# Attention, gated MLP and routed experts on one core: SyncE's transfers written into the hand-laid order, and the second pass's partial sums kept in DRAM until the third

## The chip, the cores and the metric

The kernel runs on one core of one Trainium2 chip. The metric is the device time of one execution in microseconds (us); three executions of the kernel before gave 585.97, 586.28 and 587.97 us, median 586.28.

## What is computed

Three layers follow one another on 1536 tokens (2 sequences of 768) of 512 features. The reference, cut to what matters:

```python
scores = scale * q @ k.T - slope[h] * dist            # 8 heads of 64
keep   = (pos_k < n_global) | (0 <= pos_q - pos_k < n_local)   # 8 global keys, 96 local ones
x   = softmax(where(keep, scores, -1e9)) @ v          # attention
h   = x @ w_in                                        # 512 -> 2048
x2  = (h * tanh(softplus(h))) @ w_out                 # 2048 -> 512
e   = argmax(x2 @ w_gate)                             # one of 8 experts per token
out = gate * relu(x2 @ w1[e]) @ w2[e]                 # 512 -> 1024 -> 512
```

## The kernel before, in words

**Attention.** Tokens are taken in 12 tiles of 128 (t). A step s is half a tile's heads (s = 2t or 2t+1). `a_S` makes the scores of four heads on PE (tile `sp`), `a_max` adds bias and takes the row maximum on DVE (M), `a_exp` takes the exponential on ACT (E), `a_T` transposes on PE (T, tile `pt`), `a_Tev` copies the transposes out of PSUM on ACT (C, tile `PT`), `a_V` multiplies by the values on PE (V, tile `av`). Then `a_n` scales by the row sums on DVE (N), `a_X` transposes the tile (X, tile `xp`), and `a_xh` and `a_xl` split it into a high and a low part in the rounded 32-bit type (h on ACT, l on DVE). Two tiles make a block b of 256 tokens.

**MLP.** Each product is three matmuls (high·high, high·low, low·high). The 2048 inner features are taken in 8 pairs of 128, j, and in three passes, `PASSES = [(0, 1), (2, 3), (4, 5, 6, 7)]`. A unit (pass, block, j) is a first matmul group `L1_mms` (tile `hp`, 24 matmuls), eleven small steps of `mish` (m, alternating ACT and DVE), and a second matmul group `L2_mms` (tile `acc`, 12 matmuls) that runs two units behind the first. The weights come as 64-bit floats and are converted in 32 chunks: `load_raw` (a transfer of 512 KB into tile `wst`), then `conv_raw` in parts c (three integer operations on DVE, tile `cv`), d (a cast on ACT) and e (a subtraction on DVE).

**Partial sums.** At the end of the first pass's units for a block, `acc_evac` (through `evac0`, line 506) copies the two accumulators out on ACT and SyncE writes them to DRAM (`xps`). In the second pass `part_load` (line 500) has read them back, DVE adds them to the accumulators in PSUM (line 529), and SyncE writes the sums (line 530). In the third pass they are read again and DVE adds them once more (line 522); the result goes to the router and to the expert layer.

**What sets the order.** A string of tokens, `ORDER`, lays attention, the first ten units' L1 (L), their mish steps, the first eight units' L2 (G) and 14 of the 32 conversions by hand. Inside this "loop" PE, ACT, DVE and POOL issue exactly as the tokens stand (`manual_schedule`). SyncE (SP) is not in that list: its transfers are placed by the compiler's scheduler, some called out of tokens (`scores`, `v_end`, `half1`). The buffers bound it: six staging buffers `stp` shared by query tiles and raw weights, two `vv` for the values. Each transfer on SP also waits for the eighth one before it to have landed, as eight semaphores are used in turn. After the loop the units run from a Python loop, and the scheduler orders all engines. `prefill` writes 24 pieces of zero rows into the experts' table `xg` in units 14 to 21.

The lines of that loop which the change touches:

```python
if p > 0 and j == PASSES[p][0]:
    part_load(b)
...
if u <= NU and jl == PASSES[pl][-1]:
    acc_evac(u - 2)
if 14 <= u < 22:
    for _ in range(CAPMAX // 112):
        next(zero_rows, None)
```

Of the kernel before, what the change touches and what calls it, by code (L numbers as in the profile page):

```python
# [22 lines left out]
TPB = S // 128  # L23
# [20 lines left out]
def moe_kernel(ctx, tc, q, k, v, n_global, n_local, w_in, w_out, w_gate, w1, w2, out, dbg=None):  # L44
# [12 lines left out]
    xps = dr.tile([NT, DM], F32, name="xps")  # L57
# [171 lines left out]
    def load_qk(t, n=2):  # L229
        b, i = divmod(t, TPB)  # L230
        c0 = NG + (i // 2) * KB + (i % 2) * 128
        w = n * 128
        nc.sync.dma_start(kT[:, :, c0:c0 + w], k_t[:, :, t * 128:t * 128 + w])
        qr = stp.tile([128, 4, w], F32, tag="st", name="qr")
        nc.sync.dma_start(qr, q_t[:, :, t * 128:t * 128 + w])
        for j in range(n):
            qkt[t + j] = qr[:, :, j * 128:(j + 1) * 128]

    def load_v(t):
        b, i = divmod(t, TPB)  # L240
        s0 = i * 128
        vv = at.tile([128, 2, DM], F32, tag="vv", name="vv")

        def ld(r0, n, col, tok):
            nc.sync.dma_start(vv[r0:r0 + n, col], v[b * S + tok:b * S + tok + n, :])

        if i == 0:
            ld(0, 128, 1, 0)
            nc.gpsimd.memset(vv[0:KR, 0], 0.0)
            ld(0, NG, 0, 0)  # L250
        elif i % 2 == 0:
            ld(0, NL, 0, s0 - NL)
# [141 lines left out]
    def a_xl(t):  # L394
# [8 lines left out]
        if o == 1:  # L403
            for c, xx in enumerate((xh, xl)):
                nc.sync.dma_start(xs[blk, c], xx.rearrange("p k t -> p (k t)").bitcast(F32))
# [89 lines left out]
    def part_load(b):  # L495
        xpl[b] = []
        for o in range(2):
            t = 2 * b + o
            xp = xe.tile([128, DM], F32, tag="xp", name="xpl", bufs=4)
            nc.sync.dma_start(xp, xps[t * 128:(t + 1) * 128, :])  # L500
            xpl[b].append(xp)

    def evac0(b, o):
        t = 2 * b + o
        xp = xe.tile([128, DM], F32, tag="xp", name="xpo", bufs=4)
        nc.scalar.copy(xp, accs[b][o])
        nc.sync.dma_start(xps[t * 128:(t + 1) * 128, :], xp)
        if o == 1:
            del accs[b]

    def acc_evac(u):
        p, b, j = units[u]
        if p == 0:
            evac0(b, 0)
            evac0(b, 1)
            return
        ac = accs.pop(b)
        for o in range(2):
            t = 2 * b + o
            if p == 2:  # L520
                x2 = xe.tile([128, ROW], F32, tag="x2", name="x2")
                nc.vector.tensor_add(x2[:, 0:DM], ac[o], xpl[b][o])
                nc.gpsimd.tensor_copy(x2[:, DM:DM + 1], tokid[:, t:t + 1])
                xes[t] = x2
                if "x2" in dbg:
                    nc.sync.dma_start(dbg["x2"][t * 128:(t + 1) * 128, :], x2[:, 0:DM])
            else:
                xp = xpl[b][o]
                nc.vector.tensor_add(xp, ac[o], xp)
                nc.sync.dma_start(xps[t * 128:(t + 1) * 128, :], xp)  # L530
# [75 lines left out]
    def prefill():  # L606
# [4 lines left out]
        for e in range(NE):  # L611
            for c in range(CAPMAX // 112):
                r0 = e * ERS + c * 112
                tc.keep_in_program_order(nc.sync.dma_start(xg[r0:r0 + 112, :], z))
                yield

    zero_rows = prefill()
# [234 lines left out]
    q0 b0 q1 S0 S1 M0.0 q2 M1.0 M1.1 E0.0 M0.1 S2 M0.2 E1.0 M0.3 M1.2 E0.1 M1.3 b1 E0.2 E0.3 b2 E1.1 T0.0 E1.2 c0  # L852
    T0.1 E1.3 C0.0 T1.0 C0.1 T1.1 q3 V0 M2.0 d0 c1 C1.0 S3 E2.0 C1.1 M3.0 d1 V1 M2.1 E3.0 p2 M2.2 M3.1 E2.1 M2.3
# [510 lines left out]
```

## Time and profile before

| | us |
|---|---|
| median of 3 runs | 586.28 |
| the profiled execution: its time | 586.55 |
| the profiled execution: its span, first to last instruction | 584.8 |
| PE busy | 563.5 (96% of the span) |
| DVE busy | 471.6 (81%) |
| ACT busy | 374.2 (64%) |
| the loop's last G on PE ends, and the units behind it begin | about 138 |
| the third pass ends, about | 362 |

The span and the execution's own time differ by 1.75 us, which lies around the instructions. Matmuls are pipelined, so a PE that counts as busy need not be at its full rate; the time between the starts of two rows tells more. The trace counts each 32-bit matmul of attention as two instructions, so what the order prints as x8 stands as x16 there. A few matmul records are missing, so counts in a row can be a little low.

### The profile page before, as it was taken

How to read it: one execution, taken by the hardware profiler on the slowest of the kernel's cores; microseconds unless marked ns; L12 is line 12 of the kernel's file. 1: busy time of each engine (PE TensorE's matmuls, PEld its weight loads, DVE VectorE, ACT ScalarE, POOL GpSimd, SP SyncE). 2: the span in 40 equal slices, each digit the busy share in tenths (PEclk: the TensorE clock that was granted, in tenths of full speed). 3: DMA queues.
4: the chain of work that ended last, by engine and by line, in shares of the span. 5: the costliest groups of instructions: out<-in, count | busy, mean ns of one | idle time of the engine just before them, and what ended most of it. 6: DMA issues, size and time to landing. Idle time of an engine off the chain costs nothing.

```text
span 584.8 us, 12654 instructions
## 1 busy us (share of the span) xinstructions
PE 563.5 (96%) x4650; PEld 519.9 (89%) x4650; DVE 471.6 (81%) x1141; ACT 374.2 (64%) x878; POOL 84.6 (14%) x156
## 2 busy tenths in 40 slices
PE   6998999999999998999999999899999999999994
PEld 5898899988898987999898898699999999999994
DVE  7899988899999999877776677485966778898942
ACT  6898899786666556554555645376655556776731
POOL 2204010010100100102111110122210302212111
PEclk9899999999999999999999999999999999999997
DMA  8998455556999994412232200838749276577200
GB/s 251 324 324 251 169 166 187 190 169 236 324 345 319 326 252 162 145 36 91 67 116 89 74 20 19 277 133 294 268 148 319 84 272 221 180 287 255 95 19 22
DMA packets 54654, 110.00 MB, mean 188 GB/s; under 512 B 5440, under 2 KB 12608, under 8 KB 54583
## 3 DMA queue, kind: packets, MB, share of 16 engines
q1 hardware_dynamic: 48882, 90.21, 46.7%
q0 software_dynamic: 5696, 18.89, 9.7%
q8 instruction: 38, 0.62, 0.4%
q14 instruction: 34, 0.27, 0.1%
q10 hardware_dynamic: 4, 0.00, 0.0%
HBM read 84.67 MB, written 25.10 MB: 188 GB/s over the span
## 4 chain that ended last, share of the span: by engine, by line
PE 77%; DVE 11%; DMA 4%; issue 3%; ACT 2%; SPq 1%; POOL 1%; DVEq 0%; POOLq 0%; ACTq 0%
PE hp L429 19%; PE acc L448 19%; PE bacc L721 6%; PE bhp L721 6%; PE av L367 3%; PE bacc L722 3%; PE bhp L722 3%; PE sp L301 3%; PE bhp L724 1%; PE bacc L724 1%; PE bacc L726 1%; PE bhp L725 1%; PE bacc L725 1%; PE bhp L726 1%; DMA xg<-x,dsi 1%
## 5 line engine op out<-in xcount | busy, mean ns | idle before, releaser
L448 PE MATMUL acc<-wpair,gh 128*128 128x512 f32 x384 | 120.7, 398 | 4.2 <-ACT gh L485 4.2
L429 PE MATMUL hp<-xh,wpair 128*128 128x256 f32 x768 | 118.4, 285 | 0.0
L429 PEld LDWEIGHTS hp<-xh,wpair 128*128 128x128 f32 x768 | 104.5, 188 | 3.9 <-ACT P L325 0.3
L448 PEld LDWEIGHTS acc<-wpair,gh 128*128 128x128 f32 x384 | 67.8, 188 | 16.9 <-ACT gh L485 5.4
L161 DVE TENSOR_TENSOR bw<-bst,bw 128x512 fp32r<-128x512 f32 x112 | 72.9, 685 | 10.0 <-ACT bw L160 9.5
L160 ACT CAST bw<-bst 128x512 fp32r<-128x512 f32 x112 | 64.3, 619 | 19.3 <-PE bhp L725 9.6
L448 PE MATMUL acc<-wpair,gl 128*128 128x512 f32 x192 | 74.6, 394 | 0.0
L456 ACT ACTIVATE e<-hp 128x512 f32<-128x512 f32 x48 | 28.6, 596 | 54.6 <-PE hp L429 54.6
L429 PE MATMUL hp<-xl,wpair 128*128 128x256 f32 x384 | 62.0, 282 | 0.0
L721 PE MATMUL bhp<-xc,bw 128*128 128x352 f32 (+4 forms) x192 | 59.3, 364 | 0.7 <-DVE t L756 0.6
L721 PE MATMUL bacc<-hc,bw 128*128 128x352 f32 (+4 forms) x192 | 59.2, 364 | 0.0
L429 PEld LDWEIGHTS hp<-xl,wpair 128*128 128x128 f32 x384 | 52.7, 188 | 0.8 <-issue 0.3
L722 PE MATMUL bhp<-xc,bw 128*128 128x176 f32 (+4 forms) x192 | 48.5, 253 | 0.0
L722 PE MATMUL bacc<-hc,bw 128*128 128x176 f32 (+4 forms) x192 | 48.3, 252 | 0.0
L325 ACT ACTIVATE P<-P,mx 128x232 f32<-128x232 f32 (+1 forms) x96 | 44.7, 472 | 3.1 <-DVE mx L314 2.9
L460 ACT ACTIVATE n<-e 128x512 f32<-128x512 f32 x48 | 30.4, 633 | 21.6 <-DVE e L458 19.8
L466 DVE SCALAR_TENSOR_TENSOR n<-n,r 128x512 f32<-128x512 f32 x48 | 32.9, 685 | 13.9 <-ACT r L464 13.3
L448 PEld LDWEIGHTS acc<-wpair,gl 128*128 128x128 f32 x192 | 35.7, 188 | 7.8 <-DVE gl L488 0.4
L488 DVE SCALAR_TENSOR_TENSOR gl<-n,gh 128x512 fp32r<-128x512 f32 x48 | 32.8, 686 | 9.4 <-ACT gh L485 8.6
L721 PEld LDWEIGHTS bhp<-xc,bw 128*128 128x128 f32 x192 | 36.1, 188 | 1.7 <-DVE t L756 0.8
L722 PEld LDWEIGHTS bhp<-xc,bw 128*128 128x128 f32 x192 | 36.7, 191 | 0.0
L722 PEld LDWEIGHTS bacc<-hc,bw 128*128 128x128 f32 x192 | 36.7, 191 | 0.0
(190 smaller groups left out, 1218.4 us busy)
## 6 DMA issues: line engine op xcount, KB each, us to landing
bst<-in_moe_w_dram SPq DMA_DIRECT2D x56, 512.0 KB, 6.4
wst<-in_moe_w_in_dram SPq DMA_DIRECT2D x16, 512.0 KB
wst<-in_moe_w_out_dram SPq DMA_DIRECT2D x16, 512.0 KB, 5.1
xh<-xs POOLq DMA_DIRECT2D x12, 512.0 KB, 5.5
xl<-xs POOLq DMA_DIRECT2D x12, 512.0 KB, 4.8
xpl<-xps SPq DMA_DIRECT2D x24, 256.0 KB, 4.4
xg<-z SPq DMA_DIRECT2D x24, 224.9 KB, 8.3
w0f<-in_moe_w_dram SPq DMA_DIRECT2D x8, 512.0 KB, 8.2
```

Of the source, the lines that this page charges most:

```text
L160: nc.scalar.copy(hi, src)
L161: nc.vector.tensor_sub(lo, src, hi.bitcast(F32))
L301: nc.tensor.matmul(sps[s][j][:, i, 0:w], lhsT=qkt[t][r, 2 * pr + i, :], rhs=kT[r, 2 * pr + i, k0:k0 + w], start=True, stop=True)
L325: nc.scalar.activation(out=Ps[s][:, q_, 0:w], in_=Ps[s][:, q_, 0:w], func=AF.Exp, bias=mxs[s][:, q_:q_ + 1], scale=-1.0, accum_out=rcs[t][ ...
L429: yield lambda f=f, kk=kk, wi=wi, xx=xx, cs=cs: nc.tensor.matmul(hp[:, f, :], lhsT=w[:, wi, kk, cs], rhs=xx[:, kk, :], start=(kk == 0 and ...
L448: yield lambda f=f, o=o, cs=cs, gi=gi, wi=wi, first=first, last=last: nc.tensor.matmul(accs[b][o], lhsT=gi[:, cs], rhs=w[:, wi, f, :], sta ...
L456: nc.scalar.activation(out=e, in_=hp, func=AF.Exp, scale=-1.0)
L460: nc.scalar.activation(out=n, in_=e, func=AF.Square)
L466: nc.vector.scalar_tensor_tensor(out=n, in0=n, scalar=0.25, in1=r, op0=ALU.add, op1=ALU.mult)
L488: nc.vector.scalar_tensor_tensor(out=gl, in0=n, scalar=-(2.0 ** -80), in1=gh.bitcast(F32), op0=ALU.mult, op1=ALU.subtract)
L721: nc.tensor.matmul(o[:, 0:2 * cap], lhsT=wh, rhs=xc, start=first, stop=False)
L722: nc.tensor.matmul(o[:, 0:cap], lhsT=wl, rhs=xh, start=False, stop=last)
```

## The change

SP joins the engines that `ORDER` lays out, and the string is written anew, with new tokens: K and Q (keys and queries of a tile or of two), W (values), w (a raw weight chunk), x (a block's high and low parts to DRAM), y (a partial sum to DRAM), z (a piece of zero rows) and u (clearing a value buffer). The opening's value buffer is cleared by DVE instead of POOL. `zero_tile` is made at token k, and all 24 zero pieces are written inside the loop instead of in units 14 to 21. `xps` has room for two partial sums per token. Both the first and the second pass copy their accumulators out on ACT and write them; nothing is loaded or added in the second pass. In the third pass `part_load` reads two tiles per half block at the third unit of four, `part_sum` adds them at the fourth, and one addition to the accumulator is left, as before.

```diff
-    xps = dr.tile([NT, DM], F32, name="xps")
+    xps = dr.tile([2, NT, DM], F32, name="xps")
...
-    def load_qk(t, n=2):
...
+    def load_k(t):
+        n = 1 if t < 2 else 2
...
+        nc.sync.dma_start(kT[:, :, c0:c0 + n * 128], k_t[:, :, t * 128:(t + n) * 128])
+
+    def load_q(t):
+        n = 1 if t < 2 else 2
+        qr = stp.tile([128, 4, n * 128], F32, tag="st", name="qr")
+        nc.sync.dma_start(qr, q_t[:, :, t * 128:(t + n) * 128])
...
+    def zero_v(t, eng):
+        vvt[t] = at.tile([128, 2, DM], F32, tag="vv", name="vv")
+        eng.memset(vvt[t][0:KR, 0], 0.0)
...
         if i == 0:
+            ld(0, NG, 0, 0)
             ld(0, 128, 1, 0)
-            nc.gpsimd.memset(vv[0:KR, 0], 0.0)
-            ld(0, NG, 0, 0)
...
+            xpl[b].append([xe.tile([128, DM], F32, tag="xp", name="xpl", bufs=4) for _ in range(2)])
+            for p, xp in enumerate(xpl[b][o]):
+                nc.sync.dma_start(xp, xps[p, t * 128:(t + 1) * 128, :])
+
+    def part_sum(b):
+        for x0, x1 in xpl[b]:
+            nc.vector.tensor_add(x0, x0, x1)
...
+    def evac_store(p, b, o):
+        t = 2 * b + o
+        nc.sync.dma_start(xps[p, t * 128:(t + 1) * 128, :], evs.pop((b, o)))
+
     def acc_evac(u):
         p, b, j = units[u]
-        if p == 0:
-            evac0(b, 0)
-            evac0(b, 1)
+        if p < 2:
+            for o in range(2):
+                evac0(b, o)
+                evac_store(p, b, o)
             return
...
-                xp = xpl[b][o]
-                nc.vector.tensor_add(xp, ac[o], xp)
-                nc.sync.dma_start(xps[t * 128:(t + 1) * 128, :], xp)
...
     ORDER = """
-    q0 b0 q1 S0 S1 M0.0 q2 M1.0 M1.1 E0.0 M0.1 S2 M0.2 E1.0 M0.3 M1.2 E0.1 M1.3 b1 E0.2 E0.3 b2 E1.1 T0.0 E1.2 c0
...
+    K0 Q0 Q1 K1 Q2 q1 q0 b0 q2 S0 w0 q3 S1 S2 M0.0 M0.1 W0 E0.0 M1.0 S3 M0.2 E0.1 M1.1 M1.2 K2 E1.0 M0.3 M1.3 E0.2
...
-    with tc.manual_schedule(engines={mybir.EngineType.PE, mybir.EngineType.Activation, mybir.EngineType.DVE, mybir.EngineType.Pool}), tc.tile_pool(name="tmp0", bufs=1, side="right") as tmp0:
+    with tc.manual_schedule(engines={mybir.EngineType.PE, mybir.EngineType.Activation, mybir.EngineType.DVE, mybir.EngineType.Pool, mybir.EngineType.SP}), tc.tile_pool(name="tmp0", bufs=1, side="right") as tmp0:
...
-            if p > 0 and j == PASSES[p][0]:
+            if p == 2 and j == PASSES[p][2]:
                 part_load(b)
+            if p == 2 and j == PASSES[p][3]:
+                part_sum(b)
...
-        if 14 <= u < 22:
-            for _ in range(CAPMAX // 112):
-                next(zero_rows, None)
```

SyncE's first transfers, before the change (kT, qr and vv are keys, queries and values; wst is a raw weight chunk):

```order
L233 DMA kT<-in_k_dram 128x4x128
L235 DMA qr<-in_q_dram 128x4x128
L233 DMA kT<-in_k_dram 128x4x128
L235 DMA qr<-in_q_dram 128x4x128
L245 DMA vv<-in_v_dram 128x512
L185 DMA wst<-in_moe_w_in_dram 128x2x512 x2
L245 DMA vv<-in_v_dram 104x512
L245 DMA vv<-in_v_dram 120x512
L245 DMA vv<-in_v_dram 8x512 x2
L233 DMA kT<-in_k_dram 128x4x256
L235 DMA qr<-in_q_dram 128x4x256
```

And with the change:

```order
L233 DMA kT<-in_k_dram 128x4x128
L238 DMA qr<-in_q_dram 128x4x128 x2
L233 DMA kT<-in_k_dram 128x4x128
L238 DMA qr<-in_q_dram 128x4x256
L185 DMA wst<-in_moe_w_in_dram 128x2x512
L254 DMA vv<-in_v_dram 8x512
L254 DMA vv<-in_v_dram 128x512
L233 DMA kT<-in_k_dram 128x4x256
```

The second query tile is now third, one raw chunk stands ahead of the first values instead of two, the eight global rows of the values come first of the values, and the keys of tiles 2 and 3 follow at once.

PE's first rows of attention before (sp: S, pt: T, av: V):

```order
L301 MATMUL sp<-kT,qr 128x136 x8
L301 MATMUL sp<-kT,qr 128x232 x4
L337 MATMUL pt<-ident,P 72x128 x4
L339 MATMUL pt<-ident,P 128x128 x4
L337 MATMUL pt<-ident,P 72x128 x4
L339 MATMUL pt<-ident,P 128x128 x4
L367 MATMUL av<-vv,PT 64x64 x16
L301 MATMUL sp<-kT,qr 128x232 x4
L367 MATMUL av<-vv,PT 64x64 x16
L301 MATMUL sp<-kT,qr 128x232 x8
```

And with the change:

```order
L308 MATMUL sp<-kT,qr 128x136 x8
L308 MATMUL sp<-kT,qr 128x232 x8
L344 MATMUL pt<-ident,P 72x128 x4
L346 MATMUL pt<-ident,P 128x128 x4
L344 MATMUL pt<-ident,P 72x128 x4
L346 MATMUL pt<-ident,P 128x128 x4
L374 MATMUL av<-vv,PT 64x64 x16
L308 MATMUL sp<-kT,qr 128x232 x4
L344 MATMUL pt<-ident,P 104x128 x4
L346 MATMUL pt<-ident,P 128x128 x4
L374 MATMUL av<-vv,PT 64x64 x16
```

One more group of wide scores stands ahead of the first transposes; behind the first V comes S4 (tile 2), whose keys are the last transfer shown above.

DVE in the second pass before, a piece with one of its six pairs of additions (L529):

```order
L175 SCALAR_TENSOR_TENSOR cv<-wst,cv 128x512
L529 TENSOR_TENSOR xpl<-acc,xpl 128x512
L488 SCALAR_TENSOR_TENSOR gl<-n,gh 128x512
L211 TENSOR_TENSOR wpair_2_2947<-cv,wpair_2_2947 128x512
L529 TENSOR_TENSOR xpl<-acc,xpl 128x512
L466 SCALAR_TENSOR_TENSOR n<-n,r 128x512
```

And ACT in the second pass with the change, where the copies stand between steps of mish:

```order
L470 ACTIVATE r<-n,cqs 128x512
L519 COPY xpo<-acc 128x512
L472 ACTIVATE r<-r 128x512
L493 ACTIVATE gh<-n 128x512
L519 COPY xpo<-acc 128x512
L464 ACTIVATE e<-hp 128x512
```

All twelve of DVE's additions leave the second pass, and ACT copies twelve accumulator halves there.

## Rows read from the trace of the kernel before

**Rows 1.** Busy time by stretch: length, PE, PEld, DVE, ACT, POOL, PEclk, DMA, GB/s.
```profile
15.00:20.00 5.00, 5.00 (x58) 4.23 (x56) 3.37 (x18) 3.28 (x14) 2.04 (x2) 0.66 1.07 369
...
60.00:138.00 78.00, 77.83 (x895) 69.42 (x894) 72.08 (x196) 66.89 (x177) 4.08 (x8) 1.00 0.52 171
138.00:192.00 54.00, 54.00 (x351) 49.31 (x349) 53.88 (x99) 35.93 (x63) 4.34 (x8) 1.00 0.98 329
192.00:226.00 34.00, 31.28 (x195) 27.47 (x194) 33.95 (x62) 19.89 (x33) 3.45 (x6) 1.00 0.91 273
...
240.00:360.00 120.00, 120.00 (x917) 108.12 (x916) 86.51 (x187) 66.62 (x125) 15.77 (x25) 1.00 0.22 71
```

**Rows 2.** PE's timeline, opening: start, us, engine, line, what, [idle before <-releaser].
```profile
6.00 1.20 PE L301 MATMUL sp<-kT,qr 64*128 64x136 f32 x16
...
12.31 0.34 PE L367 MATMUL av<-vv,PT 128*64 128x64 f32 x4 [0.21 <-ACT PT L352]
14.05 1.03 PE L367 MATMUL av<-vv,PT 72*64 72x64 f32 x28 [1.40 <-DMA vv<-in_v_dram]
15.02 1.56 PE L301 MATMUL sp<-kT,qr 64*128 64x232 f32 x8
...
18.41 2.03 PE L301 MATMUL sp<-kT,qr 64*128 64x232 f32 x16
```

**Rows 3.** The chain that ended last, pieces at PE's full rate: start, us, what.
```profile
22.76 2.01 PE av L367 x64
...
30.94 1.77 PE sp L301 x16
...
80.18 0.87 PE pt L339 x8
```

**Rows 4.** ACT's timeline in the opening.
```profile
7.48 0.69 ACT L275 ACTIVATE qr<-qr,qsc 128x128 f32<-128x128 f32 x2 [1.42 <-DMA qr<-in_q_dram]
...
11.22 1.04 ACT L352 COPY PT<-pt 72x512 f32<-72x512 f32 x2
```

**Rows 5.** DVE's timeline in the opening: its wait for the two integers.
```profile
3.83 0.19 DVE L71 CAST int_f<-int_raw 1x4 f32<-1x4 int32 x1 [0.70 <-DMA int_raw<-in_n_global_dram]
```

**Rows 6.** PE's timeline inside the loop.
```profile
46.55 0.64 PE L429 MATMUL hp<-xl,wpair 128*128 128x256 f32 x4
48.85 0.66 PE L339 MATMUL pt<-ident,P 128*128 128x128 f32 x4 [1.65 <-DVE xl L398]
...
64.24 0.65 PE L385 MATMUL xp<-ident,xn 128*128 128x128 f32 x4 [0.17 <-DVE xn L378]
```

**Rows 7.** The timeline of POOL and DVE ahead of that wait.
```profile
44.69 2.22 POOL L270 TENSOR_TENSOR qr<-qr,qsc 128x512 f32<-128x512 f32 x2
...
46.05 1.41 DVE L173 SCALAR_TENSOR_TENSOR cv<-wst,cv 128x512 int32<-128x512 int32 x1
...
47.50 0.69 DVE L175 SCALAR_TENSOR_TENSOR cv<-wst,cv 128x512 int32<-128x512 int32 x1
```

**Rows 8.** The chain that ended last, second pass.
```profile
186.63 2.77 PE acc L448 x12
189.39 2.90 PE hp L429 x24
...
235.49 2.76 PE acc L448 x12
```

**Rows 9.** PE's timeline, the longest wait of the second pass.
```profile
223.94 1.19 PE L448 MATMUL acc<-wpair,gh 128*128 128x512 f32 x4 [2.10 <-ACT gh L485]
```

**Rows 10.** Line 529 alone: count, ns min/median/max, first and last start.
```profile
L529 DVE TENSOR_TENSOR xpl<-acc,xpl x12: 673/678/692, 172.1 to 234.0; 128x512 f32<-128x512 f32 x12
```

**Rows 11.** Groups of instructions: busy us, mean ns of one, idle before.
```profile
L470 DVE TENSOR_TENSOR e<-e,r 128x512 f32<-128x512 f32 x48 | 32.9, 686 | 0.7
...
L506 ACT COPY xpo<-acc 128x512 f32<-128x512 f32 x12 | 6.5, 582 | 0.0
```

**Rows 12.** The page's part 6, transfers: count, KB each, median us to landing.
```profile
xg<-z SPq DMA_DIRECT2D x24, 224.9 KB, 8.3
```

More of the change, by code (lines that the diff above doesn't have):

```diff
@@ L241, in load_v @@
         s0 = i * 128
-        vv = at.tile([128, 2, DM], F32, tag="vv", name="vv")
+        if i:
+            vvt[t] = at.tile([128, 2, DM], F32, tag="vv", name="vv")
+        vv = vvt[t]
         def ld(r0, n, col, tok):
@@ L402, in a_xl, with x_store @@
                                   xx[:, :, cs].bitcast(F32))
-        if o == 1:
-            for c, xx in enumerate((xh, xl)):
-                nc.sync.dma_start(xs[blk, c], xx.rearrange("p k t -> p (k t)").bitcast(F32))
+    def x_store(blk):
+        for c, xx in enumerate(xT[blk]):
+            nc.sync.dma_start(xs[blk, c], xx.rearrange("p k t -> p (k t)").bitcast(F32))
     def x_reload(blk):
@@ L519, in acc_evac @@
             t = 2 * b + o
[L520 to L527, printed above, removed]
-                xp = xpl[b][o]
-                nc.vector.tensor_add(xp, ac[o], xp)
-                nc.sync.dma_start(xps[t * 128:(t + 1) * 128, :], xp)
+            x2 = xe.tile([128, ROW], F32, tag="x2", name="x2")
+            nc.vector.tensor_add(x2[:, 0:DM], ac[o], xpl[b][o][0])
+            nc.gpsimd.tensor_copy(x2[:, DM:DM + 1], tokid[:, t:t + 1])
+            xes[t] = x2
+            if "x2" in dbg:
+                nc.sync.dma_start(dbg["x2"][t * 128:(t + 1) * 128, :], x2[:, 0:DM])
     dsi_ins = [None]
@@ L610, in prefill, with zero_rows @@
         nc.gpsimd.memset(z[:, DM + 1:ROW], 0.0)
[L611 to L617, printed above, removed]
+        zt.append(z)
+    def zero_rows(i):
+        e, c = divmod(i, CAPMAX // 112)
+        r0 = e * ERS + c * 112
+        nc.sync.dma_start(xg[r0:r0 + 112, :], zt[0])
     cnt = const.tile([1, NE], F32, name="cnt")
@@ L934, in moe_kernel, with first_k @@
         l2 = [L2_mms(u) for u in range(LOOPU)]
-        def v_end(s):
-            a_V(s)
-            if s % 2 and s // 2 + 2 < NTILE:
-                load_v(s // 2 + 2)
-        def scores(s):
-            a_S(s)
-            if s % 4 == 3 and 1 < s // 2 // 2 + 2 + 0 < NTILE // 2 and s > 3:
-                load_qk(2 * (s // 4) + 4)
-        def half1(c):
-            next_conv(0)
-            next_raw()
+        def first_k():
+            load_k(0)
+            prep_qk(0)
         def consts(_):
@@ L952, in consts @@
             build_consts(tmp0)
[L954 removed]
+            zero_tile()
+        todo = {
             "b": lambda a: bias(a), "q": lambda s: scale_q(int(s)), "p": lambda t: prep_qk(int(t)),
[L956 removed]
+            "S": lambda s: a_S(int(s)), "V": lambda s: a_V(int(s)), "R": lambda t: a_rec(int(t)),
             "N": lambda t: a_n(int(t)), "X": lambda t: a_X(int(t)), "h": lambda t: a_xh(int(t)),
[L958 to L959 removed]
+            "l": lambda t: a_xl(int(t)), "c": lambda c: next_conv(0), "d": lambda c: next_conv(1),
+            "e": lambda c: next_conv(2), "k": consts,
             "M": lambda s, q_: a_max(int(s), int(q_)), "E": lambda s, q_: a_exp(int(s), int(q_)),
```

102 lines of the change are left out of this document (43 added, 59 removed).

## The prediction

> **What bounds the kernel now.** I read the page's first part, which makes PE the busiest engine, then busy time by stretch, then PE's timeline and the chain of waits where a stretch showed a gap. In most stretches PE has no gap at all: from 138 to 192 and from 240 to 360 it is busy all the time, from 60 to 138 for 77.83 of 78 us [rows 1]. So a change to the order can only win what PE loses, and three places show a loss that this change touches.
>
> The first is the opening. From the first scores at 6.00 to 18.41, 12.41 us, PE does sixteen narrow scores (1.20), sixteen wide ones, sixteen transposes and 64 av instructions [rows 2]. At PE's full rate the wide scores take 1.77, the av 2.01 and the transposes 2 x 0.87 = 1.74 [rows 3], together 6.72 with the narrow ones; so 5.7 are lost. They fall in three parts. Up to 12.31: 6.31 us for 1.20 + 0.885 + 1.74 = 3.8 of work, 2.5 lost, because ACT's scalings of the second query tile begin at 7.48 and its exponentials, which the transposes wait for, last to 11.22 [rows 4]. From 12.31 to 15.02: 2.71 for 1.0 of av, 1.7 lost, mostly to the values' transfer [rows 2]. From 15.02 to 18.41: 3.39 for 0.885 + 1.0, 1.5 lost with no wait; the granted clock is 0.66 there, the mean of a stretch at 2.4 and one at 1.2 GHz [rows 1].
>
> The second is one wait inside the loop: four matmuls at 46.55 take until 48.85, where four of that kind take 2.90 / 6 = 0.48 at full rate [rows 6, 8], so 1.8 are lost. PE waits for DVE's `xl`; ahead of it a conversion step of DVE took 1.41 instead of about 0.69 beside a POOL multiply [rows 7].
>
> The third is the second pass. DVE is busy for 53.88 of 54 and 33.95 of 34 us [rows 1], and PE falls behind it: 2.72 us idle between 192 and 226, the longest wait 2.10 [rows 1, 9]. From 186.63 to 235.49, 48.86 us, PE does eight units of 2.77 + 2.88 = 5.65 [rows 8], 45.2; so 3.7 are lost.
>
> **The change, part by part.** The sum is made against the profiled execution, 586.55 us (span 584.8 and 1.75 around it); it lies 0.27 above the median of 586.28.
>
> *Second pass.* Twelve DVE additions of 0.678 go [rows 10]. They come in six pairs, one per two units, from 172.1 to 234.0; four pairs, 8 x 0.678 = 5.4 us, lie ahead of the wait that ends at 223.94 [rows 9, 10]. DVE is the late engine, so it comes 5.4 earlier at that place, more than the 3.7 that PE lost. What is late next is PE itself. ACT gets twelve copies of 0.582 [rows 11], 7.0 us, in stretches where it has 18 + 14 us free [rows 1]; behind a copy stand the next steps of mish, which gh waits for, so a part comes back as latency. I take 3.2 of the 3.7. Ends: 3.7, and 1.2, where each of the four pairs' copies delays the chain by its full 0.58 once. If ACT's cover were gone, all 7.0 us would come back.
>
> *Third pass.* Added are twelve additions of two SBUF tiles, nearest row 0.686 [rows 11], 8.2 us on DVE, which has 33 us free from 240 to 360 [rows 1], and twelve more loads of 256 KB at a DMA share of 0.22. They start at the third unit of four and are added one unit (5.65) later; the slowest kind of transfer in the page's list of issues took 8.3 [rows 12], so a load could be 2.7 late, in six blocks 16 us. DVE's in-order queue with mish behind it would wait that long; the 33 us cover it beside the 8.2. Cost 0; without cover 8.2. The second pass loses its twelve loads; a gain of 0, since DVE, not DMA, is late there.
>
> *Opening.* Up to 12.31 the pacing stays, but one more group of wide scores (0.885) is done in the gaps: 1.6 lost instead of 2.5. The second query tile is now third on SP, so its four scalings come sooner than 7.48 [rows 4] and end about when the first exponential can start. For the transfers: by 7.48 four of 256 KB had landed [rows 4], by 14.05 another 256 + 1024 + 448 + 32 = 1760 KB [rows 2], so 268 KB a us. With the change the first values end 1296 KB behind the fourth transfer, at 7.48 + 4.8 = 12.3: V0 no longer waits. But S4's keys come 512 KB later, at 14.2, when V0 has been done since 13.3: 0.9 lost instead of 1.7. The 1.5 of the low clock I leave, since PE still pauses shortly before. Gain 0.9 + 0.8 = 1.7. Ends: 3.2 without the low clock, and -0.7, if the query tile lands no earlier than 7.48 and the two further scalings (0.69) delay all exponentials. The value buffer's clearing on DVE falls into DVE's wait of 0.70 for the two integers [rows 5] and costs 0; without that wait it would cost about its length, up to 0.7.
>
> *The rest of the loop.* The wait at 46.55 hangs on one meeting of POOL's multiply and a conversion; both move. Of 1.8 I take 1.1: ahead of the sixth tile's X (64.24 [rows 6]) DVE has six conversions instead of eight, so it is less late there. The ends are 1.8, and -1.8 for one more such wait at a new place. SP's moved transfers (stores of x, zero pieces) cost PE nothing as long as loads arrive in time; the loop's DMA share is 0.52 from 60 to 138 [rows 1], and taking 5.4 MB of zeros in raises it to about 0.75 [rows 1, 12]. So 0, with the rival below.
>
> Sum: 586.55 - 3.2 - 1.7 - 1.1 = 580.55, less 0.27 for the median: **580.3 us**.
>
> **The clock, weighed.** The rows show a low clock right behind PE's pause of 1.40 us, and 1.00 in every later stretch listed [rows 1, 2]. The Trainium skill, TensorE: Matmul & The Clock Gate, Part 1, says that the throttled state is the default and activity releases it. By that rule the shorter pauses of the new opening could spare the 1.5 us, for 578.8; by the row alone they need not.
>
> **The rivals.**
> 1. *The low clock goes.* PE's first 12 us have 0.885 more work and the 1.40 wait is gone [rows 2]; against it, a pause of 0.9 remains. 580.3 - 1.5 = 578.8.
> 2. *The loop wins nothing*: ACT, with 66.89 of 78 us busy [rows 1], takes DVE's place as the late engine, and only the second pass gains. 586.3 - 3.2 = 583.1.
> 3. *The second pass does not do what is promised*: two DVE additions become two ACT copies in the same chain and PE's wait stays. The loop's 2.8 alone: 583.5. Against it speaks ACT's free time.
> 4. *Slower*: SP chokes. Behind the first zero piece (after the sixth X, about 65) to the loop's end at 138 the new tokens hold 66 transfers: 24 zeros, 15 of values, 2 of keys and queries, 9 of weights, 8 of x, 8 of partial sums. Each waits for the eighth before it, so a landing time above 8 x 73 / 66 = 8.8 us decides. The zeros' median was 8.3, though at a DMA share of 0.98 [rows 1, 12]. At 9.8 the queue needs 66 x 9.8 / 8 = 81, 8 more than it has: 586.3 + 8 - 3.2 - 1.7 = 589.4. Against it: in the loop the share is about half.
> 5. *No change*: the loop loses about as much as the second pass wins, 586.
>
> **How the numbers follow.** Forecast 0.50, rival 1 0.16, rival 2 0.14, rival 3 0.06, rival 5 0.06, rival 4 0.08. Runs of this kernel can tell about 0.3% from no change, 1.8 us. The first four cases are below 584.5, except for a twentieth of chance in the upper ends of rivals 2 and 3: faster 0.82. Same: 0.10. Slower: 0.08. The range is 576.8 to 584.5. Below it reaches all gains at once (3.7 + 3.2 + 1.8 gives 577.6) with 0.8 for small losses in the loop that I did not count; above it leaves out rivals 4 and 5 and those upper ends, 0.18.
>
> **What would show it.** Right: in the second pass DVE with gaps, PE without waits on gh; first values before 13 us; PE's first unit behind the loop at about 135 instead of 138. Wrong: PE still waiting on gh with ACT saturated (rival 3); new waits of PE on DMA or ACT in the loop (rivals 2, 4); DVE waiting for partial sums in the third pass long enough that PE waits too.

## The result and the profile after

The changed kernel takes 578.13 us (median of 4 runs, 577.47 to 579.0) against 586.12 of the kernel before: the ratio is 0.9862 with a 95% interval of 0.9833 to 0.9891. The profiled execution took 578.08 us, with a span of 576.4 instead of 584.8. Forecast were 580.3 us and a range of 576.8 to 584.5: the direction and the range held, and the gain was 8.0 us instead of 5.8 to 6.0.

Busy time by stretch in the kernel after (columns as in [rows 1]: busy us of PE, PEld, DVE, ACT, POOL, then the granted clock, the DMA share and GB/s):

```profile
15.00:20.00 5.00, 5.00 (x84) 4.29 (x83) 3.26 (x18) 4.77 (x18) 2.04 (x2) 1.00 1.01 330
60.00:138.00 78.00, 77.75 (x842) 69.84 (x841) 74.33 (x189) 66.53 (x169) 4.40 (x5) 1.00 0.83 274
138.00:192.00 54.00, 54.00 (x345) 49.05 (x344) 53.69 (x98) 38.77 (x68) 5.28 (x10) 1.00 0.75 243
192.00:246.00 54.00, 54.00 (x345) 48.66 (x344) 46.15 (x81) 34.30 (x60) 4.10 (x8) 1.00 0.41 134
```

One stretch of the kernel before, which [rows 1] show only in part:

```profile
192.00:246.00 54.00, 51.28 (x323) 45.65 (x322) 51.33 (x90) 31.77 (x52) 5.04 (x10) 1.00 0.74 226
```

Two things differ. From 192 to 246 PE is busy all the time, and DVE, which had been busy for 51 of those 54 us, now has 8 us free. And from 15 to 20 the granted clock is 1.00 instead of 0.66. The zero pieces show as a DMA share of 0.83 in the loop and 0.75 behind it.

PE's timeline in the opening, kernel after:

```profile
6.09 1.20 PE L308 MATMUL sp<-kT,qr 64*128 64x136 f32 x16
7.64 1.84 PE L308 MATMUL sp<-kT,qr 64*128 64x232 f32 x16 [0.35 <-DMA kT<-in_k_dram]
12.11 1.15 PE L374 MATMUL av<-vv,PT 128*64 128x64 f32 x32 [0.21 <-ACT PT L359]
13.48 1.05 PE L308 MATMUL sp<-kT,qr 64*128 64x232 f32 x8 [0.22 <-DMA kT<-in_k_dram]
16.56 1.84 PE L308 MATMUL sp<-kT,qr 64*128 64x232 f32 x16
```

The kernel before has two longer waits there, 1.40 for the values [rows 2] and 0.74 for the scaling of the second tile's query:

```profile
7.94 1.05 PE L301 MATMUL sp<-kT,qr 64*128 64x232 f32 x8 [0.74 <-ACT qr L275]
```

Now there are short ones of 0.2 to 0.35. By 16.56 PE has done all that it had done at 18.41 before, and eight wide scores (0.885) and eight transposes (0.87) more: 1.85 + 1.76 = 3.6 us won in these two profiles. One row is not in PE's timeline, POOL's multiplication of the third and fourth tiles' queries. In the kernel before:

```profile
16.97 2.04 POOL L270 TENSOR_TENSOR qr<-qr,qsc 128x512 f32<-128x512 f32 x2 [5.25 <-DMA wst<-in_moe_w_in_dram]
```

and after:

```profile
11.05 2.04 POOL L277 TENSOR_TENSOR qr<-qr,qsc 128x512 f32<-128x512 f32 x2
```

The third tile's scores cannot start before the first half of this row ends. In the kernel before the view puts POOL's wait down to a weight chunk, the transfer that it saw come last; that it is the query which POOL waits for, the same row shows in the run with the sums alone (next section), whose opening is that of the kernel before:

```profile
16.99 2.04 POOL L270 TENSOR_TENSOR qr<-qr,qsc 128x512 f32<-128x512 f32 x2 [5.21 <-DMA qr<-in_q_dram]
```

This query will turn out to be the opening's main term.

The chain that ended last, second pass of the kernel after, as in [rows 8]:

```profile
188.06 2.77 PE acc L456 x12
190.82 2.88 PE hp L437 x24
...
236.05 2.88 PE hp L437 x24
238.94 2.97 PE acc L456 x12
```

Nine units from 188.06 to 238.94 are 5.65 each, the full rate; before, eight units took 48.86 for 45.2. What PE waits for in the whole kernel after (us in total, times, longest):

```profile
PE warm L905 <- POOL ident masks.py:199: 1.7, 1, 1.7
PE acc L456 <- ACT gh L493: 1.4, 1, 1.4
PE bacc L791 <- ACT hf L755: 1.0, 1, 1.0
PE sp L308 <- DVE mx L321: 0.7, 1, 0.7
```

The only wait on gh is the one ahead of the last unit, at 364.65, which the kernel before has too. To divide the gain, three places of PE's timeline serve: the first matmul behind the loop, the first transpose of the third pass (the router's, for the first block), and the end. The stretch between the first two holds the whole second pass, two units ahead of it and some six behind it.

| | before | after | after, again | sums alone | loop alone |
|---|---|---|---|---|---|
| first matmul behind the loop | 138.41 | 134.19 | 135.13 | 138.08 | 134.60 |
| from there to the third pass's first transpose | 119.43 | 116.07 | 115.82 | 115.85 | 121.86 |
| from there to the span's end | 326.96 | 326.14 | 326.55 | 326.67 | 327.24 |

The last three columns are runs of the next section. Of the 8.4 us between the two spans, 4.2 come from the loop, 3.4 from the second pass and 0.8 from behind it; this last part differs by more than that between runs with the same code there (325.3 to 328.0).

### The profile page after: what moved, and what is told of

Read it like the earlier page. It is cut to its first block, busy times and chain, and to the rows that moved or that the text cites. A ratio compares the mean times of both kernels' runs of the same rounds, so it can differ in the third digit from the quotient of the medians.

```text
span 576.4 us, 12667 instructions
## 1 busy us (share of the span) xinstructions
PE 560.0 (97%) x4650; PEld 517.7 (90%) x4650; DVE 470.0 (82%) x1142; ACT 379.6 (66%) x890; POOL 82.6 (14%) x155
## 4 chain that ended last, share of the span: by engine, by line
PE 85%; DVE 7%; DMA 2%; ACT 2%; issue 2%; SPq 1%; POOL 0%; DVEq 0%; POOLq 0%; ACTq 0%
PE hp L437 24%; PE acc L456 21%; PE bacc L734 6%; PE bhp L734 6%; PE av L374 3%; PE sp L308 3%; PE bacc L735 3%; PE bhp L735 3%; DVE bw L161 2%; PE pt L344 1%; PE bhp L737 1%; PE bacc L737 1%; PE pt L346 1%; PE bacc L739 1%; PE bacc L738 1%
## 5 line engine op out<-in xcount | busy, mean ns | idle before, releaser
L493 ACT ACTIVATE gh<-n 128x512 fp32r<-128x512 f32 x48 | 30.1, 626 | 16.1 <-DVE n L489 16.1
```

The source lines that it names most:

```text
L493: nc.scalar.mul(gts[u][0], n, -(2.0 ** -80))
```

## The experiments

All were timed in turn with the kernel before, on the same chip; the intervals are those of the ratio to it.

**Each half alone.** The first run gives the kernel before only the new partial sums. The second takes them away from the changed kernel: the second pass loads, adds on DVE and stores as before.

```diff
# before, sums alone
-        if p == 0:
-            evac0(b, 0)
-            evac0(b, 1)
+        if p < 2:
+            evac0(b, 0, p)
+            evac0(b, 1, p)
...
-            if p > 0 and j == PASSES[p][0]:
+            if p == 2 and j == PASSES[p][2]:
                 part_load(b)
+            if p == 2 and j == PASSES[p][3]:
+                part_sum(b)
```

> The kernel before, with only the change to the second pass's partial sums (copied out by ACT, loaded and added in the third pass); opening, loop and zero pieces as before. Theory A (DVE's twelve additions are what PE falls behind in the second pass): 3.2 us faster (2.0 to 3.7), no PE wait on gh between 192 and 226, DVE with gaps there. Theory B (the second pass is better because the zero pieces no longer fill the DMA engines from 138 to 192, or because the new loop leaves DVE less late): 0 to 1 us faster, and PE still waits on gh.

Measured: 582.36 us, ratio 0.9918 (0.9895 to 0.9942), 4.3 us faster than the kernel before beside it (586.64). The stretches of the second pass in this run:

```profile
138.00:192.00 54.00, 54.00 (x351) 49.32 (x350) 53.84 (x99) 37.94 (x68) 4.58 (x9) 1.00 0.96 311
192.00:246.00 54.00, 54.00 (x341) 48.69 (x340) 47.42 (x83) 34.89 (x61) 4.40 (x10) 1.00 0.61 198
```

PE has no gap, although the zero pieces still fill the DMA engines to 0.96 from 138 to 192. From the loop's end to the third pass's first transpose it takes 115.85 instead of 119.43: 3.6 us. Theory B falls.

```diff
# after, loop alone
-        if p < 2:
+        if p == 0:
             for o in range(2):
                 evac0(b, o)
                 evac_store(p, b, o)
             return
...
+            if p == 1:
+                xp = xpl[b][o]
+                nc.vector.tensor_add(xp, ac[o], xp)
+                nc.sync.dma_start(xps[0, t * 128:(t + 1) * 128, :], xp)
+                continue
...
-            if p == 2 and j == PASSES[p][2]:
+            if p > 0 and j == PASSES[p][0]:
                 part_load(b)
-            if p == 2 and j == PASSES[p][3]:
-                part_sum(b)
```

> The changed kernel with the second pass's partial sums as before: loaded, added by DVE in PSUM's accumulators and stored; one load and one addition in the third pass. Opening and loop as changed. Theory A: 3.2 us slower than the changed kernel (2.0 to 3.7), and PE waits on gh again in the second pass with DVE busy all the time. Theory B: 0 to 1 us slower, since DVE enters the second pass less late and the DMA engines are freer.

Measured: 583.99 us, ratio 0.9948 (0.9930 to 0.9967): slower than the changed kernel by 5.9 us in the medians and 5.0 in the ratios, more than theory A's 3.7. PE's timeline and three stretches of this run:

```profile
206.67 1.19 PE L456 MATMUL acc<-wpair,gh 128*128 128x512 f32 x4 [0.48 <-ACT gh L493]
...
221.00 1.21 PE L456 MATMUL acc<-wpair,gh 128*128 128x512 f32 x4 [2.09 <-ACT gh L493]
```

```profile
180.00:200.00 20.00, 19.47 (x129) 17.74 (x128) 19.97 (x38) 11.73 (x20) 1.05 (x2) 1.00 0.73 253
200.00:215.00 15.00, 14.52 (x99) 13.30 (x98) 15.00 (x28) 7.89 (x15) 2.11 (x4) 1.00 0.50 161
221.00:226.00 5.00, 5.00 (x18) 4.24 (x19) 4.93 (x10) 2.53 (x5) 0.00 (x0) 0.66 0.34 113
```

DVE is busy all the time until PE's wait ends. The loop ends 3.8 us earlier than before, but the same DVE work still lies ahead of that wait, so it ends only 2.9 us earlier (221.00 against 223.94 [rows 9]); and here the clock falls behind it, 0.66 for 5 us, which costs 1.7 us if PE's work goes with the clock (an estimate, 5 x 0.34). So part of a faster loop is given back while DVE bounds the second pass: 0.9 of 3.8 us here, and the clock. Up to the third pass's first transpose the sums alone win 3.9 us in the profiles, the loop alone 1.4, both 7.6: 2.3 more than their sum, of which 1.7 are that stretch of low clock in one profile. In the medians it is 4.3, 2.7 and 8.0, a difference of 1.0, which is within the intervals. That the halves help each other is suggested by the traces, not shown by the times.

**The opening: values, clock or query.** The kernel before got its first values early, with nothing else moved; DVE clears the buffer.

```diff
# before, values early
+        zero_v(0, nc.vector)
         load_qk(0, 1)
...
             ld(0, 128, 1, 0)
-            nc.gpsimd.memset(vv[0:KR, 0], 0.0)
+            if t:
+                nc.gpsimd.memset(vv[0:KR, 0], 0.0)
             ld(0, NG, 0, 0)
```

> The kernel before, with the first value buffer cleared by DVE at the start, so that its 8 first rows go right behind the 128 (272 KB behind the fourth transfer) and not behind 1.5 MB more. Theory A (the pause of 1.40 us for the values is what the low clock follows): the first values' matmuls start at about 12.3 without a wait, the next two groups run at full rate until about 15.2, and the granted clock of 15 to 20 us is no longer 0.66. The time hardly falls all the same, by 0 to 0.8 us, because the scores behind them need the query that POOL scales from 16.97 to 19.0, as before. Theory B (the low clock comes from the pauses before that, or from something else in the opening): the values start early, but the next groups still take 1.48 and 1.91 us, and the clock stays near 0.66. Theory C (the values' transfer alone bounds the opening): 1.7 us or more are won.

Measured: 588.23 us, ratio 1.001 (0.9988 to 1.0033). PE's timeline and two stretches of this run:

```profile
12.28 1.15 PE L372 MATMUL av<-vv,PT 128*64 128x64 f32 x32 [0.21 <-ACT PT L357]
...
18.96 3.25 PE L306 MATMUL sp<-kT,qr 64*128 64x232 f32 x16 [2.99 <-POOL qr L275]
```

```profile
15.00:20.00 5.00, 2.01 (x38) 1.80 (x38) 4.42 (x17) 3.60 (x15) 2.13 (x2) 0.92 1.08 369
20.00:25.00 5.00, 5.00 (x42) 4.08 (x42) 1.38 (x8) 1.96 (x5) 1.54 (x3) 0.74 1.08 341
```

The values' wait is gone and nothing is won: PE stands still for the query instead, 2.99 us, and the low clock moves behind that pause. In this trace the query itself comes 0.9 later (POOL starts at 17.86), and the loop ends at 140.35, 1.9 later than in the kernel before. Theory C falls; theory A is right about the values and the query, but a low clock is still there, now behind the other pause. The run with the sums alone has the opening of the kernel before unchanged, and there the clock stayed at 1.00 behind a longer pause for the values:

```profile
14.22 1.03 PE L367 MATMUL av<-vv,PT 72*64 72x64 f32 x28 [1.78 <-DMA vv<-in_v_dram]
15.19 1.05 PE L301 MATMUL sp<-kT,qr 64*128 64x232 f32 x8
16.17 1.15 PE L367 MATMUL av<-vv,PT 128*64 128x64 f32 x32
18.08 1.84 PE L301 MATMUL sp<-kT,qr 64*128 64x232 f32 x16 [0.76 <-POOL qr L270]
```

With the full clock PE reaches the same scores at 18.08 instead of 18.41, and waits 0.76 for POOL's query. So of the 1.5 us that [rows 2] seem to lose to the clock, 0.33 were the clock's, or 0.5 counted from the values' arrival (14.22 against 14.05). In the changed kernel, now, the values late, and then the query late:

```diff
# after, values late
-    ... M0.0 M0.1 W0 E0.0 M1.0 S3 M0.2 E0.1 M1.1 M1.2 K2 E1.0 ...
+    ... M0.0 M0.1 E0.0 M1.0 S3 M0.2 E0.1 M1.1 M1.2 K2 W0 E1.0 ...
```

> The changed kernel, with the first values' transfers behind the 512 KB of the third tile's keys. Theory A (pause, then low clock): the values land at about 13.5 instead of before 12.1, PE pauses 1.4 us as in the kernel before, the granted clock of the stretch behind falls as there, and the time grows by 1.2 to 2.7 us. Theory B (the clock has another cause): the same pause, clock 1.00, and the time grows by 0 to 1.2 us.

```diff
# after, query late
-    K0 Q0 Q1 K1 Q2 q1 q0 b0 ... T0.0 W1 E1.2 ...
+    K0 Q0 Q1 K1 q1 q0 b0 ... T0.0 W1 Q2 E1.2 ...
```

> The changed kernel, with the transfer of the third and fourth tiles' queries (512 KB) behind the second tile's values instead of in fifth place; the values keep their place or come earlier. Theory A (what bounded the opening of the kernel before was this query, which landed at 16.97 and which POOL then multiplies for 1.02, not the values and not the clock): 2272 KB behind the second keys at about 310 KB a us it lands at about 15.0, the third tile's scores start at about 16.0 instead of 13.48, and the time grows by 2 to 3 us. Theory B (the gain of the opening is the values' early arrival and the exponentials' earlier end): the time grows by 0 to 1 us.

Measured: values late 580.62 us, ratio 0.9899 (0.9874 to 0.9923), with a pause of 0.97 and no low clock; query late 582.37 us, ratio 0.9921 (0.9893 to 0.9950). PE's timeline with the values late:

```profile
13.98 1.15 PE L374 MATMUL av<-vv,PT 128*64 128x64 f32 x32 [0.97 <-DMA vv<-in_v_dram]
```

and with the query late, with two stretches:

```profile
17.36 1.92 PE L308 MATMUL sp<-kT,qr 64*128 64x232 f32 x8 [4.34 <-POOL qr L277]
```

```profile
12.00:17.00 5.00, 1.03 (x32) 0.89 (x32) 3.72 (x17) 3.15 (x12) 0.73 (x1) 0.84 1.09 312
17.00:22.00 5.00, 4.64 (x33) 3.62 (x34) 0.00 (x0) 1.66 (x6) 3.30 (x4) 0.50 0.30 104
```

The loop ends at 135.88 with the values late, and at 140.31 with the query late, later than in the kernel before. One transfer put behind seven others takes back the whole gain of the loop, and more than theory A's 3 us of it, since a low clock follows the pause. With the values late, the trace of the changed kernel that starts alike (the last run of this section, values at 13.08, loop's end at 135.13) is 0.9 and 0.75 us ahead; against the first profile (134.19) the loop ends 1.7 later. The clock of 1.00 behind the pause is what theory B says, but the pause was 0.97 and not the 1.4 that both theories put there. The times differ by 2.3, with some 2 us of uncertainty between two ratios, which lies in theory A's range and not in B's. So what late values cost stays open between 0.75 and 2.3 us.

**Are the transfers enough?** The run with the sums alone was given the opening's transfers of the changed kernel, in the old order of the engines; with the second conversion put one tile later.

```diff
# before, sums and opening's transfers
+        load_qk(2, 2, "q")
+        next_raw()
         load_v(0)
-        next_raw()
+        load_qk(2, 2, "k")
         next_raw()
         load_v(1)
-        load_qk(2)
...
-    ... V0 M2.0 d0 c1 C1.0 S3 E2.0 C1.1 M3.0 d1 V1 ... M3.2 p3 S4 M3.3 E2.2 R0 E2.3 S5 e0 E3.2 N0 ...
+    ... V0 M2.0 d0 C1.0 S3 E2.0 C1.1 M3.0 V1 ... M3.2 p3 S4 M3.3 c1 E2.2 R0 E2.3 S5 e0 E3.2 d1 N0 ...
```

> The kernel before with two things of the change alone: the second pass's partial sums (as in the run that had only these) and the opening's transfers (queries of the third tile fifth, one raw weight chunk, the first values, keys, a second chunk, the second values), for which the second conversion on DVE and its cast on ACT stand one tile later. The rest of the order is the old one, zero pieces in units 14 to 21. Theory A (of the loop's gain most is the third tile's query): the third tile's scores start at about 15.2 to 16.5 instead of 18.1 to 18.4, the loop ends 2 to 3 us earlier than in the run with the sums alone (138.08), and the time is about 579.5 to 580.5. Theory B (the gain needs the whole new order of the loop): the loop ends less than 1 us earlier, 581.5 to 582.5.

Measured: 582.34 us, ratio 0.9926 (0.9899 to 0.9953), the same as with the sums alone (582.36). POOL's multiplication, now early, meets a conversion step of DVE, which takes 1.57 instead of 0.69, and ACT's cast and PE's second values wait behind it. DVE's and PE's timelines of this run:

```profile
12.71 1.57 DVE L175 SCALAR_TENSOR_TENSOR cv<-wst,cv 128x512 int32<-128x512 int32 x1
```

```profile
16.42 1.15 PE L375 MATMUL av<-vv,PT 128*64 128x64 f32 x32 [1.43 <-ACT PT L360]
17.50 1.84 PE L309 MATMUL sp<-kT,qr 64*128 64x232 f32 x16
```

The third tile's scores start 0.6 earlier than with the sums alone (18.08), no more, and the loop ends at 139.39 instead of 138.08. From those scores to the loop's end it takes 121.9 us, 1.9 more than with the sums alone (120.0). So the query's place is needed (the run with the query late), and in the old order it does not suffice; in the changed order POOL's row at 11.05 runs beside row maxima, ahead of the first conversion. How much of the 1.9 the conversion that stands later costs, and how much the old order, this run does not separate.

**The wait that is left in the loop.** In the first profile of the changed kernel PE waits once for DVE's row maxima, 0.74 us at 56.21. DVE's and POOL's timelines there:

```profile
54.05 1.36 DVE L211 TENSOR_TENSOR wpair<-cv,wpair 128x512 fp32r<-128x512 f32 x1
```

```profile
52.82 2.04 POOL L277 TENSOR_TENSOR qr<-qr,qsc 128x512 f32<-128x512 f32 x2 [5.37 <-DVE mx L321]
```

```diff
# after, conversion moved
-    ... m3.1 e5 T12.0 m4.1 M13.0 M13.1 T12.1 M13.2 E13.0 M13.3 L2 N5 C12.0 ...
+    ... m3.1 T12.0 m4.1 M13.0 M13.1 T12.1 M13.2 E13.0 M13.3 L2 N5 e5 C12.0 ...
```

> The changed kernel with one DVE subtraction of a weight conversion (1.36 us at 54.05 beside POOL's multiply, twice its usual length) moved behind the four row maxima and the scaling that follow it on DVE. Theory A (the wait of 0.74 at 56.21 is this one meeting): the maxima come 1.3 us earlier, PE's wait goes, the subtraction takes 0.68 behind POOL's multiply; 0.7 to 1.0 us faster. Theory B (DVE is late there as a whole): the wait shows up at one of the next steps; 0 to 0.3 us.

Measured: 578.38 us, ratio 0.9855 (0.9823 to 0.9886). The step takes 0.68 in its new place and PE's wait is gone. Theory A's cause, the meeting, is borne out by the seven traces (the first profile and six of this section) in which this part of the loop stands as in the changed kernel. The step alone takes 0.68, the two multiplications alone 2.04; PE's wait for the row maxima goes with the step:

| trace | DVE's step L211 | POOL's two multiplications | PE's wait behind |
|---|---|---|---|
| values late | 1.45 | 2.04 | 0.83 |
| query late | 1.39 | 2.04 | 0.76 |
| after | 1.36 | 2.04 | 0.74 |
| after, again | 1.33 | 2.08 | 0.71 |
| loop alone | 1.08 | 2.49 | 0.46 |
| zero pieces late | 0.73 | 2.49 | none |
| sums doubled | 0.68 | 2.56 | none |

The last of them in its trace (sums doubled, a run further down), DVE's step first and POOL's row second:

```profile
54.55 0.68 DVE L211 TENSOR_TENSOR wpair<-cv,wpair 128x512 fp32r<-128x512 f32 x1
53.57 2.56 POOL L277 TENSOR_TENSOR qr<-qr,qsc 128x512 f32<-128x512 f32 x2 [5.60 <-DVE e L466]
```

So the wait is there in some executions and not in others, and theory A's size of 0.7 to 1.0 us is that of the long waits only. From the second tile's first values (20.19) to the loop's end (134.24) it takes 114.05 us with the step moved, and 114.31 in the other run that has it moved (the last unit); without the move 114.85 and 115.11 in the two traces of the changed kernel, 115.03 with the zero pieces late, but 114.56 with the loop alone and 114.21 with the sums doubled. In the times it cannot be told from no change (the changed kernel again: 578.27, ratio 0.9857).

**The third pass's cover.** Each of the twelve additions was followed by a second one.

```diff
             nc.vector.tensor_add(x0, x0, x1)
+            nc.vector.tensor_add(x1, x0, x1)
```

> The changed kernel with each of the twelve additions of the third pass followed by one more of the same size, which overwrites the buffer no longer needed. Theory A (these additions are covered by DVE's free time): 8.2 us more of DVE work, no change (within 0.8 us). Theory B (DVE's in-order queue with the steps of mish behind it is near its limit also there): 2 to 8.2 us slower, with PE waits on gh in the third pass.

Measured: 582.43 us, ratio 0.9922 (0.9895 to 0.9949): slower than the changed kernel by 4.2 us in the medians and 3.6 in the ratios. The loss lies at one place; from the loop's end to the third pass's first transpose this run takes 120.06 us. DVE's timeline, PE's timeline and one stretch of this run:

```profile
239.69 0.69 DVE L513 TENSOR_TENSOR xpl<-xpl 128x512 f32<-128x512 f32 x1 [3.65 <-DMA xpl<-xps]
```

```profile
241.64 0.53 PE L456 MATMUL acc<-wpair,gl 128*128 128x512 f32 x1 [2.40 <-DVE gl L496]
```

```profile
240.00:246.00 6.00, 4.36 (x14) 3.51 (x15) 4.62 (x9) 2.21 (x4) 0.00 (x0) 0.72 0.15 46
```

In this profile it is not the sum of DVE's work that costs: a load that landed late stood at the head of DVE's queue with the steps of mish behind it, PE waited 2.40, and the low clock behind the pause made it about 4.2. In the changed kernel DVE waits for these loads too, 6.0 us in seven waits of at most 2.3 (3.6 in the second trace), and PE does not notice. Its longest wait is for the same addition:

```profile
237.99 0.69 DVE L513 TENSOR_TENSOR xpl<-xpl 128x512 f32<-128x512 f32 x1 [2.32 <-DMA xpl<-xps]
```

This is the third of the twelve additions, so it belongs to the second block, whose sum is not used before 271.98 (L538); the scheduler has put it ahead of steps that PE needs at once. Its load can only be issued when an earlier addition has freed one of four buffers: at 233.45 in the changed kernel, at 233.73 in this run, where the second addition holds the buffer longer. From there to the addition's start it takes 4.5 us in the changed kernel, 2.6 in its second trace and 6.0 here. So the doubling delays the load by 0.3 directly; why the landing took longer here no run shows, but all seven times of this run (581.15 to 583.49) lie above the changed kernel's. Theory A's "covered by free time" holds for the changed kernel alone.

**The zero pieces** were put back behind the loop, three each in units 14 to 21.

```diff
+        if 14 <= u < 22:
+            for i in range(3 * (u - 14), 3 * (u - 13)):
+                tc.keep_in_program_order(zero_rows(i))
```

> The changed kernel with the 24 zero pieces back in units 14 to 21, outside the loop. Theory A (neither stage is bound by transfers): no change (within 0.8 us), with the DMA share of 60 to 138 back near 0.5 and that of 138 to 192 near 0.97. Theory B (the pieces in the loop delay loads there): 1 us or more faster. Theory C (in the second pass they would delay the weight chunks): 1 us or more slower.

Measured: 579.93 us (578.25 to 584.78), ratio 0.9898 (0.9861 to 0.9935), which just includes the changed kernel's first ratio (0.9862) and not its second (0.9857). The loop's end (135.03) and the second pass (115.85) lie within the two traces of the changed kernel; the DMA share is 0.59 in the loop and 0.91 behind it. B falls; between A and a small loss the times leave it open.

**The last unit.** The changed kernel with the moved conversion, and the last unit's first group ahead of the second group of two units earlier.

```diff
-            phase_(rt, jl, 0, L1_mms(u))
+            phase_(rt, jl, 0, L1_mms(u) if u < NU - 1 else iter(()))
+            if u == NU - 2:
+                run_mms(L1_mms(NU - 1), 99)
```

> The changed kernel with the moved conversion and, at the end of the third pass, the last unit's first matmul group one group earlier, so that its eleven steps have 2.8 us more before the last accumulation. Theory A (the wait of 1.43 us on gh there is latency alone): it goes, 1.0 to 1.4 us faster than with the moved conversion alone. Theory B (the expert layer's first transfers or the router's steps take its place as the late one): 0 to 0.4 us.

Measured: 583.13 us, ratio 0.9948 (0.9928 to 0.9967), 4.9 us slower than the changed kernel on the same chip. The wait on gh is gone, and behind it PE waits for the expert layer's first rows, with a low clock behind that:

```profile
370.93 1.33 PE L721 MATMUL btp<-ident,xr 128*128 128x128 f32 x5 [4.73 <-DMA xr<-xg]
```

```profile
371.00:383.00 12.00, 11.51 (x74) 9.78 (x75) 3.61 (x20) 4.15 (x13) 1.25 (x6) 0.52 0.63 230
```

The group went ahead of the router's matmuls, whose result that load waits for: they run at 353.68 instead of 350.37. Theory A's wait went and its gain did not come; theory B named the transfer that takes its place, but not a loss of 4.9. The gap of 1.43 was the cheaper place.

**The changed kernel again**, on the chip of the run with the last unit early.

> The changed kernel as it is, beside the other two on the same chip: 577.5 to 579 us by its first runs. How far its opening differs from its first profile (scores at 6.09, third tile's scores at 16.56, loop's end at 134.19) shows what of the differences of the other runs is the execution's and not the kernel's.

Measured: 578.27 us, ratio 0.9857 (0.9833 to 0.9881). Its opening differs from that of the first profile. PE's timeline:

```profile
6.74 4.54 PE L308 MATMUL sp<-kT,qr 64*128 64x136 f32 x32
...
17.24 1.84 PE L308 MATMUL sp<-kT,qr 64*128 64x232 f32 x16
```

So places in the opening vary between executions, and the opening's gain is 3.6 us by the first profile and 2.9 by this one. Five more runs of this section have the same opening (loop alone, zero pieces late, conversion moved, sums doubled, last unit early); there the row of 17.24 starts between 17.07 and 17.86. The first profile's 16.56 is the earliest of the seven, and 2.9 is the better value.

## Why the prediction was right, and where it was not

*Second pass*: right. Forecast were 3.2 us with an end at 3.7; 3.4 and 3.6 came (119.43 against 116.07 and 115.82). Sums alone and loop alone bear out both the size and DVE as the cause. The latency behind ACT's copies, for which half a microsecond was taken off, does not show. (The lower end, 1.2, does not follow from its own working: four copies of 0.58 off 3.7 leave 1.4.)

*Third pass*: right at 0. From its first transpose to the last but one PE takes 98.68 us, 98.66 before. But the working counted on 33 us of free DVE time, and what matters is how late a load stands ahead of mish: 2.3 us were covered, and in the run with the sums doubled 3.65 cost 4.2. The loads were late, as was feared, but not by a landing time of 8.3: they wait for buffers, and the scheduler placed some additions well ahead of their unit.

*Opening*: the mechanism was half right, and this is the step that failed: 1.7 us were forecast, with 3.2 as the upper end, and 2.3 to 3.6 came, in five of seven traces 2.8 to 3.1. The prediction followed the values and the third tile's keys through the transfers, but not that tile's query, which in the kernel before POOL begins to multiply at 16.97. It took what PE lost from 15.02 to 18.41 for the clock's and left it. The runs show the clock's part as 0.3 to 0.5; at the full clock PE would have waited for this query instead, whose transfer the change moves to fifth place. The earlier exponentials (0.9) and the values (0.8) came about as said: V0 at 12.11 with one more group of wide scores behind it, and no wait for the values.

*Rest of the loop*: 1.1 us were forecast, and the loop's end less the opening leaves 0.4 to 0.6 in the two traces of the changed kernel (3.3 - 2.9, 4.2 - 3.6). The wait at 46.55 went, and one of the same kind came at 56.21, again POOL's multiplication beside a conversion step, in five of seven traces. In the four traces without that wait it is 1.1 to 1.4 three times and 0.4 with the zero pieces late, where PE waits 0.49 for row maxima at another place (75.52). The sizes fit the ends that were given. The errors of opening and loop lie in opposite directions, so that their sum, 2.8 forecast and 3.3 to 4.2 measured, is nearer than its parts: that is luck.

*The rivals.* Rival 1's time, 578.8, is the nearest to the measured one, for a reason that did not hold: the clock did stay up, but that alone is worth 0.3 to 0.5. By the rule that was weighed there (the Trainium skill, TensorE: Matmul & The Clock Gate, Part 1: the throttled state is the default, activity releases it) the short pauses could leave the clock up; the traces agree in that each low stretch stands behind a pause, and do not tell which pauses do it. Rival 2's price for the second pass alone, 583.1, and rival 3's for the loop alone, 583.5, are close to what the halves took, 582.36 and 583.99, though neither case came. SP did not choke (rival 4), though the loop's DMA share came to 0.83 and not 0.75: up to the third pass's end PE waits for a transfer twice in the first profile, 0.35 and 0.22, both in the opening.

*Behind the third pass's first transpose* 0.4 to 0.8 us were won that nothing forecast. Since runs with the same code there take from 325.3 to 328.0, this part is no gain that a run shows.

## What to carry to other kernels

In an opening that transfers pace, follow every operand of the next three or four steps to its landing, and through the engine that prepares it: taking away the wait that shows only moves PE to the next late operand. A faster stage ahead of one that another engine bounds can give part of its gain back there (0.9 of 3.8 us in the one trace here); lighten that stage in the same change. Before a wait of half a microsecond is called a property of the order, look for it in several executions. An in-order engine that waits for a load is judged by how late the load is and what stands behind it, not by the engine's free time.

## What had not been expected of the hardware

The low clock follows pauses of PE, but not each of them. Pauses and the granted clock right behind, from the traces:

| pause of PE, us | run and place | granted clock behind it |
|---|---|---|
| 0.97 | values late, 13.98 | 1.00 |
| 1.40 | before, 14.05 | 0.66 from 15 to 20 |
| 1.43 | after, 364.65, and sums and opening's transfers, 16.42 | 1.00 |
| 1.65 | before, 48.85 [rows 6] | 1.00 |
| 1.78 | sums alone, 14.22 | 1.00 |
| 2.09 | loop alone, 221.00 | 0.66 from 221 to 226 |
| 2.10 | before, 223.94 | 1.00 |
| 2.40 | sums doubled, 241.64 | 0.72 from 240 to 246 |
| 2.99 | before with values early, 18.96 | 0.74 from 20 to 25 |
| 4.34 | query late, 17.36 | 0.50 from 17 to 22 |
| 4.73 | last unit early, 370.93 | 0.52 from 371 to 383 |

The same pause in the same code, 1.4 to 1.8 at the values and 2.1 in the second pass, gave both. So one profile's low stretch is no property of the kernel, and a price for it from one profile is a guess.

In the second trace of the changed kernel the first 32 scores take 4.54 us; in the first they take 1.20 + 1.84 and a wait of 0.35. The granted clock reads 1.00 in both. Of nine traces that begin with these 32 scores, six take 4.5 to 4.8 and three 2.9 to 3.4. Why, is open.

A POOL multiplication of two SBUF tiles and a DVE step with two SBUF inputs lengthen each other, and which of them pays differs between executions of the same order. In the table of seven traces above DVE's step takes from 0.68 to 1.45, and POOL's two multiplications 2.56 where the step kept its 0.68. Other DVE steps with two SBUF inputs that met one took 1.41 [rows 7] and 1.57 instead of 0.69. A step with one SBUF input was lengthened too, from 0.42 to 0.98, in the kernel before, beside the row of 44.69 in [rows 7]:

```profile
45.04 0.98 DVE L171 TENSOR_SCALAR cv<-wst 128x512 int32<-128x512 int32 x1
```

In the stretch of the changed kernel that holds the step of 1.36, two DVE steps with an input from PSUM kept their length:

```profile
52.85 0.68 DVE L405 TENSOR_TENSOR xl<-xp,xh 128x512 fp32r<-128x512 f32 x1
53.45 0.68 DVE L489 TENSOR_TENSOR n<-e,hp 128x512 f32<-128x512 f32 x1
```

The Trainium skill, GPSIMD Engine Reference, section 1, says that GpSimd's SBUF interfaces are shared with VectorE, with contention where the DVE instruction is in a 2-port performance mode or has two SBUF inputs. The rows with two SBUF inputs agree; whether the step with one input runs in such a mode no run here shows.
